# Four Strassen units moved ahead of the third block's up products, and second products of five groups by seven Strassen products

## The chip, the cores and the metric

The program runs on one core of a Trainium2 chip. The metric is the device time of one execution in microseconds (us), as a median of several runs. Inside the core, TensorE (PE) multiplies matrices into eight PSUM banks, VectorE (DVE) and ScalarE (ACT) read the banks and prepare operands, GpSimd (POOL) issues the accumulating transfers, and SyncE (SP) issues the other ones.

## The reference

The kernel computes one transformer block on x of 2048 tokens by 512 features in float32: layer norm with a modulation, an FNet mixing step, a gated residual, a second modulated layer norm (LN2), a SwiGLU with a hidden width of 1792, and a second gated residual. Cut to what matters here:

```python
h = layernorm(x) * (1 + scale1) + shift1
a, b = h @ dft_hid_re.T, h @ dft_hid_im.T
x = x + gate1 * (dft_seq_re @ a - dft_seq_im @ b)
h = layernorm(x) * (1 + scale2) + shift2
out = x + gate2 * ((silu(h @ w1) * (h @ w3)) @ w2)
```

The change touches only the last line and the order of the work around it.

## The kernel before, in words

Every float32 product is made of three matmuls on halves: each operand is split into a high half (a rounded copy, made on ACT by `copy`, line 87) and a low half (what the rounding left, made on DVE by `minus`, line 90), and `product` (line 98) issues high by high, high by low and low by high into one PSUM bank; all matmuls of the SwiGLU stand at line 100.

The tokens are cut into four blocks t of 512, which go in two pairs, (0, 2) and (1, 3). The hidden width is cut into seven groups of 256, each with its parts of w1, w3 and w2. So there are fourteen pieces of work, a group for a pair of blocks.

- Groups 0 and 1 of the first pair are done plainly. `up_block` (line 1076) issues 12 matmuls for one half of a group's columns and one block. It takes the banks 0 to 3 in turn. Block 0 comes first, then its second products, and then block 2, whose LN2 (`ln2`, line 817) has to be done by then.
- The other twelve pieces are `items` (line 1160): i = 0 to 4 are groups 2 to 6 of the first pair, i = 5 to 11 are groups 0 to 6 of the second pair. Their products with w1 and w3 are made by seven Strassen products each, called a1 to a7 (w1) and b1 to b7 (w3). `factor` (line 1239) issues one of them, six matmuls that may accumulate on in a bank that was already copied out; ACT (line 87) and DVE (line 93) take the partial results out. `weight_jobs` makes the sums of weight parts that the products need, and splits the weights and the sums into halves.
- `result` (line 1219) makes silu(a) times b and splits it into the tiles hf, of which there are four for a piece (two blocks by two halves of the columns).
- The second products (hf by w2) are made by `down_unit` (line 1115): for one block t and one of four output chunks d, six matmuls into a bank. ACT scales the bank by the gate into half of a tile y (line 335), and for every second chunk POOL issues a DMA that adds y, 512 KB, to the tile `sums[t, d // 2]` in the chip's memory (line 1146). The slot of y is given back four units later. That makes four such DMAs for a piece.
- For groups 5 and 6 of the second pair no y is made: `load_sums` (line 1103) has read the sums back into the tiles xr through SP, DVE adds the bank into xr (line 1137), and after group 6 SP stores xr as the output (line 1141). `load_sums` stands at the end of the second products of group 4 of the second pair, for one block after the other.

The order of the units is written out as strings in the loop over `items` (lines 1656 to 1670): "a6" is a unit of this item, "-b7" one of the item before, and "y" takes the next second product from the queue `seconds`. For most items it is

```python
body = "a6 a5 y a7 y y a4 y a3 y b1 y b2 y b6 b5 y"
head = "-b7 a1 -b4 -b3 a2 " if i == turning else "-b7 a1 a2 -b4 -b3 " if i else "a1 a2 "
```

`unit` (line 1621) and `down` (line 1579) issue one unit each, and with some of them loads of the next weights (`load_w`, line 1032, on SP). After each unit, `beside` (line 1566) takes steps from the queue `jobs` (weight splits and sums), and from `background` (LN2, the sums of LN2's parts) when `jobs` is empty, as far as DVE and ACT are thought to have time. `drain` (line 132) takes steps until a named one is done; `behind` (line 1063) puts something off by so many units. Each engine works through its instructions in the order in which they were issued. Tiles come from 50 slots of 512 KB that are taken first in, first out. `judge` (line 1003) is a short test on DVE of the inputs, 12 small instructions.

Of the kernel before, what the change touches and what calls it, by code (L numbers as in the profile page):

```python
# [42 lines left out]
def folded(nc, pools, c, cp, wmr, wmc, x, xt, ctr, cti, wdr, wdi, w1, w3, w2, out):  # L43
# [1032 lines left out]
    def up_block(g, t, q, w):  # L1076
        if q == 0 and w == "w1":
            drain(lambda: ("h2", t, 1) in done)
        to = bank(turn[0] % 4)
# [33 lines left out]
    down_banks = [4, 4]  # L1113

# [49 lines left out]
    def weight_jobs(i, w):  # L1164
# [30 lines left out]

        step(jobs, 1, highs, 0.0, 1.0)
        step(jobs, 1, totals, 1.4)
        step(jobs, 1, lows, 1.2)
        step(jobs, 1, sum_highs, 0.0, 1.0)
# [9 lines left out]
    state, vs = {}, {}  # L1209

# [8 lines left out]
    def result(i, w, q, k, src):  # L1219
# [6 lines left out]
        times(v, v, src)  # L1226

# [9 lines left out]
        behind(2, lows)  # L1237

    def factor(i, w, n):
# [37 lines left out]
        if n == 3:  # L1277
            for x in wuse.pop(key).values():
                give(x)
            behind(1, lambda: give(st["x"]))  # L1280
            if w == "w3":
                for x in vs.pop(i):
                    behind(3, lambda x=x: give(x))
# [295 lines left out]
    def down(g, pair, t, d, key):  # L1579
        drain(lambda: (key, "l") in done, jobs)  # L1580
        delayed()
        down_unit(g, pair, t, d, key)
        beside(1.36, USED["own" if pair == 1 and g >= NG - 2 else "y"])

    for w in ("w1", "w3"):
        load_w((w, 1))
        plain_jobs((w, 1))
    up(0, 0)
    for g in range(2):
        load_w(("w2", g))  # L1590
        plain_jobs(("w2", g))
    up(1, 0)
    load_w(("w1", *items[0]))
    for g in range(2):
        for d in range(ND):
            down(g, 0, 0, d, ("w2", g))
    judge()
    up(0, 2)
    load_w(("w3", *items[0]))
    weight_jobs(0, "w1")  # L1600
    up(1, 2)
    for h in (h2h, h2l):
        give(h.pop((2, 0)))


    down_banks[:] = [6, 2]
# [13 lines left out]

    def unit(kind, i, n):
        g, pair = items[i]
        more = i + 1 < len(items)
        if n == 1:
            drain(lambda: ("ready", i, "w1" if kind == "a" else "w3") in done, jobs)
# [8 lines left out]
        if (kind, n) == ("a", 1) and more:  # L1634
            load_w(("w1", *items[i + 1]))
        if (kind, n) == ("a", 6):
            load_w(("w2", g, pair))
        if (kind, n) == ("a", 3) and more:
            load_w(("w3", *items[i + 1]))
            weight_jobs(i + 1, "w1")  # L1640
        if (kind, n) == ("b", 2):
            plain_jobs(("w2", g, pair))
        if (kind, n) == ("b", 3):
# [7 lines left out]
            if more:  # L1651
                weight_jobs(i + 1, "w3")
            for t in PAIRS[pair]:
                seconds.extend((g, pair, t, d, ("w2", g, pair)) for d in range(ND))
        beside(1.36, FACTOR[kind][n])

    weight_jobs(0, "w3")
    ln2(1)
    ln2(3)
    for i in range(len(items)):  # L1660
        body = "a6 a5 y a7 y y a4 y a3 y b1 y b2 y b6 b5 y"
        if i == turning:
# [3 lines left out]
        head = "-b7 a1 -b4 -b3 a2 " if i == turning else "-b7 a1 a2 -b4 -b3 " if i else "a1 a2 "  # L1666
# [813 lines left out]
```

## Time and profile before

| | us |
|---|---|
| median of 3 runs | 711.03 |
| lowest and highest run | 710.54, 712.84 |
| the profiled execution's own time | 708.46 |
| its span, first to last instruction | 706.7 |
| PE busy | 686.3 (97% of the span) |
| DVE busy | 548.3 (78%) |
| ACT busy | 430.8 (61%) |
| POOL busy | 119.4 (17%) |

The page's time is that of one profiled execution; it lies 2.57 us under the median of the runs. PE's busy time includes matmuls at a lower clock; the mean granted clock over the span is 0.991. The duration of one matmul in the rows includes its filling and draining, and matmuls overlap: the pitch from one start to the next is what counts for a sum. The SwiGLU's Strassen part begins near 320 us and lasts to the end.

### The profile page before, as it was taken

The page shows a single profiled execution, that of the slowest core. Times are in us where ns is not written, and L with a number is a line of the kernel's source. Part 1 is how long each engine was busy: PE and PEld are TensorE (multiplying, and loading weights), DVE is VectorE, ACT ScalarE, POOL GpSimd, SP SyncE. Part 2 cuts the span into 40 slices and gives each one's busy share as a digit, 9 for nine tenths or more (in the row PEclk, how much of TensorE's full clock was granted, in tenths as well). Part 3 has the DMA queues.
Part 4 walks back from the last instruction along what each step waited for, and adds up shares of the span by engine and source line. Part 5 has one row for each costly group of instructions (what it writes and reads, how often), then busy time and mean ns, then how long its engine had stood idle before and what let it go on. Part 6 is the DMA issues. An engine that isn't in the chain of part 4 may idle for free.

```text
span 706.7 us, 8912 instructions
## 1 busy us (share of the span) xinstructions
PE 686.3 (97%) x3152; PEld 564.7 (80%) x3152; DVE 548.3 (78%) x877; ACT 430.8 (61%) x709; POOL 119.4 (17%) x141
## 2 busy tenths in 40 slices
PE   7999999999999999899999999999999999999995
PEld 4898888888888888687888788787788888888784
DVE  5999679997999978579987886896865556664763
ACT  4998865545454655745677676867665565656420
POOL 1320253542524000200100101011010100101000
PEclk9999999999999999999999999999999999999998
DMA  8730299796678521522868558376763847537403
GB/s 266 211 120 1 77 373 328 251 307 229 207 283 287 168 86 41 92 58 64 209 114 199 89 130 153 61 156 137 239 136 73 180 62 175 111 69 162 137 0 124
DMA packets 38100, 108.93 MB, mean 154 GB/s; under 512 B 4896, under 2 KB 5152, under 8 KB 38048
## 3 DMA queue, kind: packets, MB, share of 16 engines
q0 software_dynamic: 12352, 43.00, 29.3%
q1 hardware_dynamic: 25264, 63.98, 27.5%
q10 hardware_dynamic: 432, 1.31, 0.5%
q8 instruction: 26, 0.43, 0.3%
q14 instruction: 26, 0.21, 0.1%
HBM read 76.81 MB, written 33.55 MB: 156 GB/s over the span
## 4 chain that ended last, share of the span: by engine, by line
PE 81%; DVE 7%; ACT 6%; issue 2%; DMA 2%; SPq 1%; ACTq 0%; DVEq 0%
PE bank L100 52%; PE bank L750 25%; PE bank L559 2%; PE bank L598 1%; DMA wmr<-in_wmr 1%; ACT xc L894 1%; PE bank L576 1%; DVE xc L96 1%; SPq L231 1%; ACT hf L87 1%; ACT y L335 1%; DVE v L96 0%; DVE hl L90 0%; ACT hm L501 0%; DMA w<-in_wdi 0%
## 5 line engine op out<-in xcount | busy, mean ns | idle before, releaser
L100 PE MATMUL bank<-hf,w2h 128*128 128x512 f32 (+1 forms) x452 | 140.9, 391 | 0.3
L1146 POOL DMA_DIRECT2D sum<-y x48 | 41.0, 855 | 390.1 <-ACT y L335 373.0
L100 PEld LDWEIGHTS bank<-hf,w2h 128*128 128x128 f32 x452 | 84.3, 188 | 22.1 <-DVE hf L90 3.4
L100 PE MATMUL bank<-hf,w2l 128*128 128x512 f32 (+1 forms) x226 | 87.6, 388 | 0.0
L87 ACT ACTIVATE hf<-v 128x512 fp32r<-128x512 f32 x56 | 35.3, 630 | 67.3 <-DVE v L96 62.7
L335 ACT ACTIVATE y<-bank,gb 128x512 f32<-128x512 f32 x96 | 64.9, 682 | 18.6 <-PE bank L100 18.3
L93 DVE TENSOR_TENSOR v<-bank,x 128x512 f32<-128x512 f32 x36 | 24.7, 685 | 34.9 <-PE bank L100 34.8
L750 PE MATMUL bank<-bh,us 128*128 128x512 f32 x128 | 49.9, 390 | 0.0
L93 DVE TENSOR_TENSOR x<-bank,x 128x512 f32<-128x512 f32 x36 | 24.7, 687 | 32.4 <-PE bank L100 28.7
L750 PE MATMUL bank<-bh,ul 128*128 128x512 f32 x128 | 49.8, 389 | 0.0
L750 PE MATMUL bank<-d,us 128*128 128x512 f32 x128 | 49.8, 389 | 0.0
L750 PE MATMUL bank<-d,uh 128*128 128x512 f32 x128 | 49.8, 389 | 0.0
L750 PE MATMUL bank<-l,us 128*128 128x512 f32 x128 | 49.8, 389 | 0.0
L750 PE MATMUL bank<-l,uh 128*128 128x512 f32 x128 | 49.8, 389 | 0.0
L100 PEld LDWEIGHTS bank<-hf,w2l 128*128 128x128 f32 x226 | 42.4, 188 | 8.4
L90 DVE TENSOR_TENSOR hf<-v,hf 128x512 fp32r<-128x512 f32 x56 | 38.5, 687 | 12.2 <-ACT hf L87 12.1
L170 POOL DMA_INDIRECT re<-in_ctr,mirror x32 | 35.8, 1117 | 66.2 <-DVE ul L90 39.5
L1224 ACT ACTIVATE v<-v 128x512 f32<-128x512 f32 x36 | 22.8, 632 | 38.8 <-DVE v L93 38.8
L87 ACT ACTIVATE x<-bank 128x512 f32<-128x512 f32 x72 | 41.4, 586 | 7.2 <-PE bank L100 6.5
L170 POOL DMA_INDIRECT im<-in_cti,mirror x32 | 32.7, 1023 | 35.3 <-PE bank L750 10.0
L100 PE MATMUL bank<-h2h,w1h 128*128 128x512 f32 x80 | 31.8, 397 | 1.5 <-ACT h2h L87 1.5
L100 PE MATMUL bank<-h2l,w1h 128*128 128x512 f32 x80 | 31.9, 399 | 0.8 <-DVE h2l L90 0.8
(246 smaller groups left out, 1775.2 us busy)
## 6 DMA issues: line engine op xcount, KB each, us to landing
sum<-y POOLq DMA_DIRECT2D x48, 512.0 KB, 5.6
w<-in_w SPq DMA_DIRECT2D x42, 512.0 KB, 4.5
re<-in_ctr SPq DMA_DIRECT2D x32, 256.0 KB, 5.0
im<-in_cti SPq DMA_DIRECT2D x32, 256.0 KB, 5.0
wmc<-in_wmc SPq DMA_DIRECT2D x8, 512.0 KB, 6.3
xr<-in_xt SPq DMA_DIRECT2D x8, 512.0 KB, 7.6
sum<-xr SPq DMA_DIRECT2D x8, 512.0 KB, 6.2
x<-in_x SPq DMA_DIRECT2D x11, 256.0 KB, 4.8
```

What stands on the lines that cost most here:

```text
L87: nc.scalar.activation(dst, src, AF.Copy, scale=scale)
L90: nc.vector.tensor_tensor(out=dst, in0=a, in1=b, op=OP.subtract)
L93: nc.vector.tensor_tensor(out=dst, in0=a, in1=b, op=OP.add)
L96: nc.vector.tensor_tensor(out=dst, in0=a, in1=b, op=OP.mult)
L100: nc.tensor.matmul(acc, lhs[a], rhs[b], start=first and n == 0, stop=last and n == len(PASSES) - 1, skip_group_check=more,)
L170: nc.gpsimd.indirect_dma_start(dst, None, rows, bass.IndirectOffsetOnAxis(ap=at, axis=0))
L231: queue.dma_start(raw_w[dt][q * 64 : (q + 1) * 64, m, :], w[i][par::2, q])
L335: nc.scalar.activation(dst, src, AF.Identity, scale=by)
L559: nc.tensor.matmul(halves(hb[k])[:, m, :], sides((hh, hl)[a][k])[:, dt, m, :], wu[dt][:, b, m, :], start=False, stop=dt % 2 == 1 and n == ...
L750: nc.tensor.matmul(acc[what, e], lhs, rhs, start=begin and i == 0, stop=(end or (turn and what == "x")) and i == len(terms) - 1, skip_grou ...
L1146: nc.gpsimd.dma_start(sums[t, d // 2], y, accum_op=OP.add)
L1224: behind(k != 0 or q == 0, lambda: nc.scalar.activation(v, src, AF.Silu))
```

## The change

It has two parts. First, the units a1, a2, b1 and b2 of the first Strassen item are issued ahead of the up products of block 2, with w1's and w3's raw halves made early and the sums of weight parts later; `judge` comes after them, and the up products of block 2 take the banks 1, 2, 4 and 5. Second, for groups 0 to 4 of the second pair (`SEVEN`, i = 5 to 9) the second products of both blocks are made by seven Strassen products of six matmuls (`seven_unit`) instead of eight units of six. Each of the seven writes two banks, 6 and 7 (three matmuls each); four of them (3, 6, 7 and 4) accumulate on in the same two banks after ACT copied them out. Each of the seven gives one y and one accumulating DMA. The operands need four more subtractions on DVE and seven split tiles instead of four (`seven_parts`), and sums of parts of w2 (`seven_jobs`).

The order strings change with it: the seven products of an item stand two units apart. The w3 jobs of the items ahead of a `SEVEN` item follow b6 instead of b3. `load_sums` for both blocks now stands after the last of the seven products of group 4, which is in the head of the last item. The core of the diff:

```diff
+    def seven_parts(i, q, k):
...
+        t1, t2, t3, t4 = v[0, 0], v[1, 1], v[0, 1], v[1, 0]
+        behind(1, lambda: minus(t1, v[0, 1], v[0, 0]))
+        behind(2, lambda: high(5, t1))
+        behind(2, lambda: minus(t3, v[1, 1], v[0, 1]))
+        behind(3, lambda: low(5, t1))
+        behind(3, lambda: minus(t2, v[1, 1], t1))
+        behind(4, lambda: high(7, t3))
+        behind(4, lambda: minus(t4, v[1, 0], t2))
...
+    def seven_unit(g, pair, n, key):
+        new = n in (1, 2, 5)
+        if new:
+            banks7[:] = [bank(6), bank(7)]
+        y = take(F32, "y")
...
+        for e, to in enumerate(banks7):
+            at = int(LEFT7[n][1]) * HALF + e * P
+            product(
+                to,
+                [flat(wuse[key][x])[:, at : at + P] for x in names],
+                [u[:, b, :] for b in range(2)],
+                new,
+                True,
+                not new,
+            )
+            d = 2 * which + e
+            copy_by(y[:, e, :], to, gb[:, d : d + 1])
+        give(u)
+        nc.gpsimd.dma_start(sums[t, which], y, accum_op=OP.add)
+        behind(4, lambda: give(y))
...
+            if g == NG - 3:
+                for t in PAIRS[pair]:
+                    load_sums(t)
...
+    for at in ("a1", "a2", "b1", "b2"):
+        unit(at[0], 0, int(at[1]))
     judge()
+    up_banks[:] = 1, 2, 4, 5
+    down_banks[:] = [6, 2]
     up(0, 2)
...
         body = "a6 a5 y a7 y y a4 y a3 y b1 y b2 y b6 b5 y"
+        if i and items[i - 1] in SEVEN:
+            body = "a6 a5 a7 y a4 a3 y b1 b2 y b6 b5 y"
+        spread = i > 1 and items[i - 2] in SEVEN
+        if spread and i < len(items) - 1:
+            body = body.replace("a6", "a6 y", 1)
...
-            body = "a6 a5 y a7 y y a4 y a3 b1 y b2 b6 b5 y b7 y b4 y b3 y y y y y y y y"
...
+            body = "a6 a5 a7 a4 a3 b1 b2 y b6 y b5 y b7 y b4 y y b3 y y y y y y y y y y"
...
+        if spread and i < len(items) - 1:
+            head = "-b7 a1 y a2 -b4 y -b3 "
+        if i == len(items) - 1:
+            head = "-b7 y a1 a2 y -b4 -b3 y "
```

How the order of instructions moves at three places follows. In these rows a name's first number counts tiles, and the x at the end says how many instructions one row stands for.

First DVE, at LN2 of block 2, before:

```order
L90 TENSOR_TENSOR hf_379_2737<-v_377_2714,hf_379_2737 128x512
L883 RECIPROCAL s_2_377_2721<-s_2_377_2721 32x16
L847 COPY w_2_382_2753<-s_2_377_2721 32x16 x4
L848 STREAM_TRANSPOSE stat_347_2556<-w_2_382_2753 128x512
L96 TENSOR_TENSOR xc_348_2564<-xc_348_2564,stat_347_2556 128x1024
L96 TENSOR_TENSOR xc_360_2611<-xc_360_2611,stat_347_2556 128x1024
L90 TENSOR_TENSOR h2l_393_2821<-xc_348_2564,h2h_392_2819 128x1024
```

and now (w1l and w3l are the low halves of the first Strassen item's weights):

```order
L90 TENSOR_TENSOR hf_379_2737<-v_377_2714,hf_379_2737 128x512
L90 TENSOR_TENSOR w1l_388_2774<-w1_380_2740,w1h_387_2772 128x1024
L90 TENSOR_TENSOR w3l_391_2787<-w3_381_2742,w3h_390_2785 128x1024
L883 RECIPROCAL s_2_377_2721<-s_2_377_2721 32x16
L847 COPY w_2_391_2790<-s_2_377_2721 32x16 x4
L848 STREAM_TRANSPOSE stat_347_2556<-w_2_391_2790 128x512
L96 TENSOR_TENSOR xc_348_2564<-xc_348_2564,stat_347_2556 128x1024
L96 TENSOR_TENSOR xc_360_2611<-xc_360_2611,stat_347_2556 128x1024
L93 TENSOR_TENSOR v_400_2846<-bank1_402_2849,x_399_2845 128x512
L90 TENSOR_TENSOR h2l_404_2859<-xc_348_2564,h2h_403_2857 128x1024
L90 TENSOR_TENSOR h2l_408_2873<-xc_360_2611,h2h_407_2871 128x1024
```

The two weight splits now stand ahead of the reciprocal, and one addition of a Strassen unit stands ahead of the first low half of block 2.

Then ACT at the same place, now, from the last scaled copies of block 0 on (h2h are the high halves of block 2; line 1252 is the silu of a Strassen item):

```order
L335 ACTIVATE y_395_2815<-bank7_397_2827,gb_152 128x512
L894 ACTIVATE xc_360_2611<-xc_360_2611,sb_150,cb1_151 128x512 x2
L87 ACTIVATE x_399_2845<-bank0_398_2838 128x512
L87 ACTIVATE h2h_403_2857<-xc_348_2564 128x1024
L1252 ACT_TABLE_LOAD
L1252 ACTIVATE v_400_2846<-v_400_2846 128x512
L87 ACTIVATE x_406_2869<-bank3_405_2862 128x512
L87 ACTIVATE h2h_407_2871<-xc_360_2611 128x1024
```

Before, nothing but one scaled copy stood between the two h2h; now a table load, a silu and a copy of a Strassen unit do.

Last, the queue of SP near the end, before:

```order
L1106 DMA xr_903_5645<-sum_1_0_3300 128x1024
L1106 DMA xr_904_5646<-sum_1_1_3302 128x1024
L1035 DMA w3_905_5656<-in_w3 128x1024
L1106 DMA xr_925_5749<-sum_3_0_3799 128x1024
L1106 DMA xr_926_5750<-sum_3_1_3801 128x1024
L1035 DMA w2_937_5818<-in_w2 128x1024
```

and now:

```order
L1035 DMA w3_934_5753<-in_w3 128x1024
L1106 DMA xr_968_5933<-sum_1_0_3380 128x1024
L1106 DMA xr_969_5934<-sum_1_1_3382 128x1024
L1106 DMA xr_970_5937<-sum_3_0_3831 128x1024
L1106 DMA xr_971_5938<-sum_3_1_3833 128x1024
L1035 DMA w2_974_5953<-in_w2 128x1024
```

All four reads of the sums now stand together, after the last w3 and directly ahead of the last w2, the one of group 6. On DVE the low half of that w2 stands ahead of the first addition into xr:

```order
L90 TENSOR_TENSOR w2l_982_6009<-w2_974_5953,w2h_981_6007 128x1024
L1138 SCALAR_TENSOR_TENSOR xr_968_5933<-bank6_984_6013,gb_152,xr_968_5933 128x512
L90 TENSOR_TENSOR hf_983_6011<-v_959_5874,hf_983_6011 128x512
L1138 SCALAR_TENSOR_TENSOR xr_968_5933<-bank7_985_6029,gb_152,xr_968_5933 128x512
L1138 SCALAR_TENSOR_TENSOR xr_969_5934<-bank6_988_6046,gb_152,xr_969_5934 128x512
```

Here bank6 is used again by the third of the units whose results are added into xr.

## Rows read from the trace of the kernel before

**Rows 1.** The page, busy time of each engine over the span.
```profile
PE 686.3 (97%) x3152; PEld 564.7 (80%) x3152; DVE 548.3 (78%) x877; ACT 430.8 (61%) x709; POOL 119.4 (17%) x141
```

**Rows 2.** The critical chain, 225 to 320 us: start, duration, what.
```profile
262.54 21.77 PE bank L100 x96
...
297.97 22.07 PE bank L100 x90
```

**Rows 3.** PE's timeline, 294 to 325 us: start, duration, what, count [idle before].
```profile
294.80 0.39 PE L100 MATMUL bank<-hf,w2l 128*128 128x512 f32 x1
296.71 0.51 PE L100 MATMUL bank<-h2h,w1h 128*128 128x512 f32 x1 [1.53 <-ACT h2h L87]
297.97 0.79 PE L100 MATMUL bank<-h2l,w1h 128*128 128x512 f32 x1 [0.76 <-DVE h2l L90]
...
301.96 0.40 PE L100 MATMUL bank<-h2h,w3h 128*128 128x512 f32 x1
...
324.11 0.50 PE L100 MATMUL bank<-th,w1sh 128*128 128x512 f32 x1 [0.23 <-ACT x L87]
```

**Rows 4.** Windows: stretch, us, busy PE, PEld, DVE, ACT, POOL, clock, DMA.
```profile
28.00:29.00 1.00, 0.30 (x3) 0.10 (x1) 0.94 (x5) 1.00 (x3) 0.84 (x2) 1.00 0.61 201
298.00:299.00 1.00, 1.00 (x3) 0.81 (x4) 0.79 (x1) 0.98 (x2) 0.37 (x1) 0.50 0.97 193
547.46:577.63 30.17, 30.17 (x134) 24.70 (x133) 17.85 (x27) 18.25 (x28) 3.40 (x5) 1.00 0.60 122
```

**Rows 5.** ACT's timeline around LN2 of block 2.
```profile
287.29 1.82 ACT L335 ACTIVATE y<-bank,gb 128x512 f32<-128x512 f32 x3
290.49 1.53 ACT L894 ACTIVATE xc<-xc,sb,cb 128x512 f32<-128x512 f32 x2 [1.37 <-issue]
295.61 1.05 ACT L87 ACTIVATE h2h<-xc 128x1024 fp32r<-128x1024 f32 x1
298.20 1.28 ACT L1094 ACT_TABLE_LOAD   x1
```

**Rows 6.** DVE's timeline: around LN2 of block 2, and from 660 to 666 us.
```profile
287.42 0.24 DVE L883 RECIPROCAL s<-s 32x16 f32<-32x16 f32 x1 [0.93 <-ACT s L880]
289.18 2.36 DVE L96 TENSOR_TENSOR xc<-xc,stat 128x1024 f32<-128x1024 f32 x2
296.69 1.23 DVE L90 TENSOR_TENSOR h2l<-xc,h2h 128x1024 fp32r<-128x1024 f32 x1 [5.15 <-ACT h2h L87]
...
660.97 0.42 DVE L93 TENSOR_TENSOR w3s<-w 128x256 f32<-128x256 f32 x1
...
665.91 0.74 DVE L1137 SCALAR_TENSOR_TENSOR xr<-bank,gb,xr 128x512 f32<-128x512 f32 x1
```

**Rows 7.** Groups by shape, 547.46 to 577.63 us: count, busy, mean ns, idle before.
```profile
L335 ACT ACTIVATE y<-bank,gb 128x512 f32<-128x512 f32 x9 | 6.2, 685 | 2.3 <-PE bank L100 2.3
L90 DVE TENSOR_TENSOR hf<-v,hf 128x512 fp32r<-128x512 f32 x4 | 2.7, 686 | 0.7 <-ACT hf L87 0.7
L87 ACT ACTIVATE hf<-v 128x512 fp32r<-128x512 f32 x4 | 2.5, 634 | 4.6 <-DVE v L96 3.4 <-issue 1.3
```

**Rows 8.** Accumulating transfers, 288 to 345 us, from issue to landing.
```profile
DMA to landing us min/median/max: 5.3/5.6/8.6
```

**Rows 9.** POOL's timeline near the end.
```profile
653.82 0.85 POOL L1146 DMA_DIRECT2D sum<-y  x1 [5.95 <-ACT y L335]
```

**Rows 10.** SP's DMA queue, 659 to 661 us.
```profile
659.62 0.32 SPq L1106 DMA_DIRECT2D xr<-sum  x1
660.04 0.38 SPq L1035 DMA_DIRECT2D w<-in_w  x1
```

**Rows 11.** DMA issues, 659 to 661 us: count, KB each, us to landing.
```profile
xr<-sum SPq DMA_DIRECT2D x1, 512.0 KB, 3.6
w<-in_w SPq DMA_DIRECT2D x1, 512.0 KB, 4.4
```

**Rows 12.** ACT's timeline at the last w2.
```profile
674.33 1.05 ACT L87 ACTIVATE w2h<-w 128x1024 fp32r<-128x1024 f32 x1
```

More of the change, by code (lines that the diff above doesn't have):

```diff
@@ new lines, in seven_jobs, with highs, totals, lows @@
+    def seven_jobs(key):
+        use = wuse[key] = {}
+        def highs():
+            use["h"] = take(F32R, "w2h")
+            copy(flat(use["h"]), flat(wraw[key]))
+        def totals():
+            use["s"] = take(F32, "w2s")
+            s, r = four(use["s"]), four(wraw[key])
+            plus(s[:, 0, :], r[:, 1, :], r[:, 3, :])
+            minus(s[:, 1, :], s[:, 0, :], r[:, 0, :])
+            minus(s[:, 2, :], r[:, 0, :], r[:, 1, :])
+            minus(s[:, 3, :], r[:, 2, :], s[:, 1, :])
+        def lows():
+            use["l"] = take(F32R, "w2l")
+            r = wraw.pop(key)
+            minus(flat(use["l"]), flat(r), flat(use["h"]).bitcast(F32))
+            give(r)
+        def sum_highs():
+            use["sh"] = take(F32R, "w2sh")
+            copy(flat(use["sh"]), flat(use["s"]))
+        def sum_lows():
+            use["sl"] = take(F32R, "w2sl")
+            minus(flat(use["sl"]), flat(use["s"]), flat(use["sh"]).bitcast(F32))
+            give(use.pop("s"))
+            done.add((key, "l"))
+        step(jobs, 1, highs, 0.0, 1.0)
+        step(jobs, 1, totals, 1.4)
+        step(jobs, 1, lows, 1.2)
+        step(jobs, 1, sum_highs, 0.0, 1.0)
+        step(jobs, 1, sum_lows, 1.2)
@@ L1577, in up, with down @@
                 beside(2.72, USED[w])
-    def down(g, pair, t, d, key):
+    def down(g, pair, *which):
+        key = which[-1]
         drain(lambda: (key, "l") in done, jobs)
         delayed()
-        down_unit(g, pair, t, d, key)
+        if (g, pair) in SEVEN:
+            seven_unit(g, pair, *which)
+        else:
+            down_unit(g, pair, *which)
         beside(1.36, USED["own" if pair == 1 and g >= NG - 2 else "y"])
[L1585 to L1606, printed above, removed]
     seconds = deque((g, 0, 2, d, ("w2", g)) for g in range(2) for d in range(ND))
@@ L1623, in unit @@
         more = i + 1 < len(items)
-        if n == 1:
-            drain(lambda: ("ready", i, "w1" if kind == "a" else "w3") in done, jobs)
+        w = "w1" if kind == "a" else "w3"
+        if n == 1 or (i, n) == (0, 6):
+            need = ("raw", w) if (i, n) == (0, 1) else ("ready", i, w)
+            drain(lambda: need in done, jobs)
         if (kind, i, n) == ("a", 0, 6):
@@ L1633, in unit @@
         factor(i, "w1" if kind == "a" else "w3", n)
-        if (kind, n) == ("a", 1) and more:
+        if (kind, n) == ("a", 1 if i else 6) and more:
             load_w(("w1", *items[i + 1]))
@@ L1637, in unit @@
             load_w(("w2", g, pair))
[L1638 removed]
+        if (kind, n) == ("a", 7 if i == turning else 3) and more:
             load_w(("w3", *items[i + 1]))
             weight_jobs(i + 1, "w1")
[L1641 to L1642 removed]
+        if (kind, n) == ("b", 2 if i else 6):
+            (seven_jobs if (g, pair) in SEVEN else plain_jobs)(("w2", g, pair))
         if (kind, n) == ("b", 3):
@@ L1650, in unit @@
                 other_operands()
-            if more:
+            if more and not early_w3(i):
                 weight_jobs(i + 1, "w3")
-            for t in PAIRS[pair]:
-                seconds.extend((g, pair, t, d, ("w2", g, pair)) for d in range(ND))
-        beside(1.36, FACTOR[kind][n])
-    weight_jobs(0, "w3")
+            if (g, pair) in SEVEN:
+                seconds.extend((g, pair, n, ("w2", g, pair)) for n in ORDER7)
+            else:
+                for t in PAIRS[pair]:
+                    seconds.extend((g, pair, t, d, ("w2", g, pair)) for d in range(ND))
+        if (kind, n) == ("b", 6) and more and early_w3(i):
+            weight_jobs(i + 1, "w3")
+        beside(1.36, FACTOR[kind][n])
+    for w in ("w1", "w3"):
+        load_w((w, 1))
+        plain_jobs((w, 1))
+    up(0, 0)
+    for g in range(2):
+        load_w(("w2", g))
+        plain_jobs(("w2", g))
+    up(1, 0)
+    for w in ("w1", "w3"):
+        load_w((w, *items[0]))
+        weight_jobs(0, w)
+    for g in range(2):
+        for d in range(ND):
+            down(g, 0, 0, d, ("w2", g))
+    for at in ("a1", "a2", "b1", "b2"):
+        unit(at[0], 0, int(at[1]))
+    judge()
+    up_banks[:] = 1, 2, 4, 5
+    down_banks[:] = [6, 2]
+    up(0, 2)
+    sum_jobs("w1")
+    up(1, 2)
+    for h in (h2h, h2l):
+        give(h.pop((2, 0)))
+    sum_jobs("w3")
     ln2(1)
```

61 lines of the change are left out of this document (58 added, 3 removed).

## The prediction, made before the changed kernel was run

> **What bounds the kernel now.** I read the busy time of the engines first: PE works for 97% of the span [rows 1], so the time is nearly the number of matmuls by their pitch, plus the places where PE waits. The chain of waits confirms this: both long pieces of it around LN2 of block 2 are matmuls at line 100 [rows 2]. The first of them gives the pitch, 21.77 / 96 = 0.2268 us for a matmul, 1.36 us for a unit of six. PE's timeline then shows where PE waits in the SwiGLU: at one place for long, between the second products of block 0 and the up products of block 2, and later only for small pieces such as the 0.23 us at 324.11 [rows 3]. The windows by stage show one group of the second pair, 30.17 us in which PE never rests while DVE works for 17.85 us and ACT for 18.25 [rows 4]. So in that stage a matmul less is time won, as long as DVE and ACT keep up.
>
> **Base.** The sum is made against the profiled execution (708.46 us, span 706.7). It lies 2.57 us under the median of the runs, 711.03. I carry the difference over to the median. A measurement of this kernel can tell about 0.3% from no change, which is 2.1 us here: below 708.9 is faster, above 713.2 slower.
>
> **Term 1, matmuls.** Eight units of six become seven in five groups: 5 x 6 = 30 matmuls fewer. At 0.2268 us [rows 2] that is **-6.8 us**. PE has no idle time in a group of the second pair [rows 4], so all of it counts if nothing new makes PE wait.
>
> **Term 2, LN2 of block 2.** Before, the last matmul of the second products starts at 294.80, and the 13th of the up products, the first with w3h, at 301.96 [rows 3]. Without any wait that one would start at 294.80 + 13 x 0.2268 = 297.75. So 4.2 us are lost there. Some 2.7 of them are idle (1.68 ahead of the first matmul, 1.03 ahead of the second), and 1.5 the clock: the 11 matmuls from 297.97 took 3.99 us instead of 2.49 [rows 3], under a granted clock of 0.50, which is the lower of its two levels, 1.2 GHz; it fell after the first wait [rows 4].
>
> The change gives PE 24 matmuls more ahead of that wait, 5.4 us, to 300.5. But the LN2 is late too. The two splits w1l and w3l now stand ahead of the reciprocal on DVE, and each waits for its high half on ACT. ACT's three scaled copies end at 289.1 [rows 5]. Then come w1h (1.05, as for the equally large h2h [rows 5]), a scaled copy of 0.6, and w3h until 291.6; DVE's w3l (1.23, as for the equally large h2l) ends at 292.9, and the reciprocal follows at 292.9 instead of 287.42 [rows 6]. From there the two products with the statistics begin 1.7 us later and last 2.36 [rows 6]; ACT's scalings (0.76 each), with one copy of y and one of x between, end at 299.9, and the first h2h at 300.9, its low half at 302.2. On ACT the table load (1.28 [rows 5]), a silu and a copy of x now stand ahead of the second h2h, which ends at 304.3, and its low half at 305.6. The up products need these at their 1st, 2nd, 7th and 8th matmul. So the 8th starts at 305.6, where it could have been at 302.05: 3.55 us are lost, in pieces of 0.5 to 1.0. Whether the clock falls for such pieces, no row shows exactly: it did after 1.68 us, at a cost of 1.5, and did not after 0.70 us in one us [rows 4]. I take 0.5, because the pieces are nearest to the second row, with 0 and 1.5 as ends. With the 0.23 at 324.11, which goes since a1 is done early, the term is 3.55 + 0.5 - 4.2 - 0.2 = **-0.4 us**, between -0.9 and +0.8. The first part of the change moves the gap rather than closing it. The splits cost nothing by themselves; they are work that stood later.
>
> **Term 3, the groups with seven products.** PE needs 30.17 x 126/132 = 28.8 us for such a group. DVE gets three more low halves and four subtractions (0.686 each, [rows 7]), four sums of w2's parts (0.42 each, as for w3s [rows 6]) and a split of 1.23: 17.85 + 7.7 = 25.5 us, 89%. ACT gets six scaled copies (0.685), three high halves (0.634) [rows 7] and one of 1.05: 18.25 + 7.1 = 25.3 us, 88%. Neither becomes the bound, but the slack shrinks from 12 us to 3.5. The products stand two units apart, so both banks have 2.72 us to be copied out, in which ACT needs 1.37 and what stands ahead. I followed the order of ACT and DVE against PE's through one group at these durations: the tightest place, bank 6 between products 6 and 7, has some 0.4 us to spare, and at the first such item DVE is some 0.8 us late with the sum after a7, for which a4 waits. I take 0.8 + 4 x 0.1 = **+1.2 us**, with ends 0 (all hidden) and +3. The three accumulating transfers more for a group are behind nothing that PE waits for, unless a y's slot is missing: it is given back four units after the issue, 5.4 us, taken again later, and transfers landed after 5.6, at worst 8.6 us [rows 8].
>
> **Term 4, the last item.** Here the change adds a wait. The four reads of the sums now follow the last seven product of group 4, and the load of the last w2 is queued behind them on SP. Let z be the end of that product on PE. ACT has a high half ahead, then copies both banks until z + 2.1; POOL issues y. The second read, of `sum_1_1`, needs it landed: before, a y issued at 653.82 released such a read at 659.62 [rows 9, 10], 5.8 us later, so z + 7.9 here. Behind it stand two more reads and w2, issued 0.42 apart [rows 10]. A read lands after 3.6 us and a w2 issued 0.42 behind it after 4.4, so they land 1.22 us apart [rows 10, 11]: w2 lands at z + 7.9 + 3.6 + 3 x 1.22 = z + 15.2. Then w2h on ACT, 1.05 [rows 12], its low half on DVE, 1.23, and only then, in DVE's order, the first addition into xr, 0.74 [rows 6], which frees bank 6: z + 18.2. PE wants that bank for the third unit of its kind, whose place is eleven units after z, 15.0 us. So PE waits 3.2 us, and the clock falls as it did after 1.68 us, 1.5 more: **+4.8 us** (ends 1.5, if the reads run side by side and the clock holds, and 6). Before, the same w2 landed at 660.04 + 4.4 = 664.4 and was first used at 674.33 [rows 10 to 12]: 10 us to spare, all of which go.
>
> The Trainium skill, DMA: Bandwidth & Descriptors, section Anatomy of one DMA, gives for a transfer issued by the other path about 2.0 us plus bytes by 436 KB per us. By it, as an estimate, four of 512 KB in a row would take 6.8 us instead of 7.3, PE would wait 0.5 less, and the sum be 0.5 lower. The rows are of the queue in question and decide.
>
> **Sum.** -6.8 - 0.4 + 1.2 + 4.8 = -1.2 us, which gives 709.8. With all ends low it is -6.8 - 0.9 + 0 + 1.5 = -6.2 (704.8), all high +3.0 (714.0). The forecast's own range is 707.4 to 712.2.
>
> **Rivals.**
> - The tail hides its wait: the reads of the sums don't hold w2 up that long, or DVE's order leaves the addition in front. Terms 1 to 3 remain, -6.0: **705.0**. For it: the 5.8 us between issue and read may hold a wait of SP for something else. Against: SP's queue in the order of the change has w2 last. Chance 0.22.
> - The gap at LN2 closes altogether, for instance if DVE's splits run before the reciprocal's wait is over: 3.9 us better than term 2 at most, the rest as forecast: **705.7**. Against: w3h stands behind four scaled copies on ACT. Chance 0.06.
> - Slower: the two banks of the seven products are not emptied in time. All seven use banks 6 and 7, and four go on in the very bank that ACT has just read. If one weight split of 1.05 us more than I foresee stands ahead of the copies at two products of a group, PE waits 2 x (1.05 - 0.4) = 1.3 us in each of the four steady groups: 5.2, so +4.0 and **715.0**. It decides from about 0.9 us a group on. For it: ACT and DVE at 88 to 89%. Against: the spacing of two units. Chance 0.14. The Trainium skill, Perfetto Trace Analysis, section Matmuls, speaks for this rival: independent groups of matmuls should rotate through banks so that one's evacuation lies beside the next one's matmuls. By it every group would pay some such wait; no row of before shows a second product going on in a bank just copied.
> - The forecast: 0.58, of which faster 0.20, same 0.34, slower 0.04.
>
> **Numbers.** Faster 0.20 + 0.22 + 0.06 = 0.48; same 0.34 + 0.02 of the slower rival = 0.36; slower 0.04 + 0.12 = 0.16. The range is 704.8 to 714.0: it takes in both faster rivals and the high end, and leaves out most of the slower one.
>
> **What would show it.** In the profile after: 1848 matmuls at line 100 instead of 1878; the reciprocal near 292.9 and matmuls of the first up unit in pieces until 306; a group of 28.8 to 29.2 us with PE full; a wait of about 3 us on DVE at line 1138 with w2l before it, in the last 35 us, and a clock below 1.00 there. I am wrong if PE runs through the last item, if the group is over 29.7 us, or if the up products start without a wait.

## The result, and the profile after

The changed kernel takes 712.99 us (median of 22 runs, 708.80 to 715.38), the kernel before 710.20 us (22 runs beside them, 708.27 to 712.84). The ratio is 1.0032, with a 95% interval from 1.0022 to 1.0043: slower, by some 2.3 us (the two medians lie 2.8 apart; the changed kernel's runs spread more widely). The forecast was 1.2 us faster.

Three rows of the page of the changed kernel answer to [rows 1]: the number of matmuls fell by 30, and PE's share of the span fell with it, so PE waits more.

```profile
span 711.1 us, 9006 instructions
...
PE 681.3 (96%) x3122; PEld 558.9 (79%) x3122; DVE 582.8 (82%) x937; ACT 454.9 (64%) x759; POOL 132.3 (19%) x156
...
PEclk9999999999999999999999999999999999999998
```

To see where the time went, one can follow the matmuls of the SwiGLU one by one. The first up product and the last second product are these, in PE's timeline of the kernel before (start, duration, what):

```profile
262.38 0.39 PE L100 MATMUL bank<-h2h,w1h 128*128 128x512 f32 x1
...
698.47 0.28 PE L100 MATMUL bank<-hf,w2l 128*128 128x256 f32 x1
```

and in that of the changed kernel, with those of the waits between them on which the readings below rest (the idle time ahead of a matmul and what ended it stand in brackets):

```profile
263.99 0.39 PE L100 MATMUL bank<-h2h,w1h 128*128 128x512 f32 x1
...
303.63 0.50 PE L100 MATMUL bank<-h2l,w1h 128*128 128x512 f32 x1 [0.76 <-DVE h2l L90]
305.74 0.50 PE L100 MATMUL bank<-h2h,w1h 128*128 128x512 f32 x1 [0.69 <-ACT h2h L87]
307.00 0.50 PE L100 MATMUL bank<-h2l,w1h 128*128 128x512 f32 x1 [0.76 <-DVE h2l L90]
...
334.81 0.73 PE L100 MATMUL bank<-hf,w2h 128*128 128x512 f32 x2 [0.54 <-ACT y L335]
336.94 0.50 PE L100 MATMUL bank<-th,w1h 128*128 128x512 f32 x1 [0.47 <-DVE v L93]
...
344.62 0.74 PE L100 MATMUL bank<-hf,w2h 128*128 128x512 f32 x2 [0.58 <-ACT y L335]
...
515.65 0.50 PE L100 MATMUL bank<-th,w1h 128*128 128x512 f32 x1 [1.04 <-DVE v L93]
...
564.95 0.73 PE L100 MATMUL bank<-hf,w2sh 128*128 128x512 f32 x2 [0.16 <-ACT y L335]
...
659.77 0.50 PE L100 MATMUL bank<-th,w1sh 128*128 128x512 f32 x1 [0.68 <-ACT x L87]
662.28 0.50 PE L100 MATMUL bank<-th,w1h 128*128 128x512 f32 x1 [0.85 <-DVE v L93]
677.78 1.22 PE L100 MATMUL bank<-hf,w2h 128*128 128x512 f32 x2 [4.33 <-DVE xr L1138]
...
702.76 0.28 PE L100 MATMUL bank<-hf,w2l 128*128 128x256 f32 x1
```

So the SwiGLU takes 436.09 us before and 438.77 after, 2.68 more. (The 1.61 us by which it starts later belong to a part of the program that the change doesn't touch; the last section returns to them.) Thirty matmuls at 0.2267 us are 6.80 us less, so 9.48 us more are lost. For each stretch, the lost time is the time between the starts of its first matmul and of the next stretch's, less the number of its matmuls times 0.2267 us:

| stretch | lost before, us | lost after, us | difference |
|---|---|---|---|
| LN2 of block 2, to the ninth up product | 4.19 | 3.44 | -0.75 |
| the rest up to the end of the first Strassen item | 0.73 | 2.50 | +1.77 |
| the other items of the first pair, up to the first units of the second | 4.06 | 2.38 | -1.68 |
| up to the second of the seven products (the wait at 515.65 is in it) | 0.77 | 1.32 | +0.55 |
| from there on, the groups with seven products | 0.96 | 3.01 | +2.05 |
| the last item | -0.17 | 7.37 | +7.54 |

The loss includes idle time, the slower start of a matmul after it and the lower clock; in the last item, matmuls of half the width make it a little less. The rows above show the places. The long wait of [rows 3] became three short ones at the 2nd, 7th and 8th up product, as forecast, and three waits in the first Strassen item (334.81 to 344.62) are new. A group with seven products costs little (0.16 to 0.25 us of wait at bank 6 in each). The row at 677.78 is the one that decides: PE waits 4.33 us for the first addition into xr, 4.5 with the slower start of its first matmul. The chain behind it, backwards, is in four views. DVE's timeline (the first two rows are from LN2 of block 2, for a later section):

```profile
291.70 1.23 DVE L90 TENSOR_TENSOR w1l<-w,w1h 128x1024 fp32r<-128x1024 f32 x1 [3.60 <-ACT w1h L87]
...
294.37 0.23 DVE L883 RECIPROCAL s<-s 32x16 f32<-32x16 f32 x1
...
675.83 1.23 DVE L90 TENSOR_TENSOR w2l<-w,w2h 128x1024 fp32r<-128x1024 f32 x1 [5.94 <-ACT w2h L87]
676.98 0.75 DVE L1138 SCALAR_TENSOR_TENSOR xr<-bank,gb,xr 128x512 f32<-128x512 f32 x1
```

ACT's timeline:

```profile
674.75 1.06 ACT L87 ACTIVATE w2h<-w 128x1024 fp32r<-128x1024 f32 x1 [7.46 <-DMA w<-in_w]
```

SP's queue, with the three later reads in one row, and POOL's, with the last accumulating transfer:

```profile
653.84 0.33 SPq L1106 DMA_DIRECT2D xr<-sum  x1
...
665.86 1.27 SPq L1106 DMA_DIRECT2D xr<-sum  x3
...
667.23 0.38 SPq L1035 DMA_DIRECT2D w<-in_w  x1
```

```profile
658.58 0.85 POOL L1360 DMA_DIRECT2D sum<-y  x1 [3.89 <-DVE hf L90]
```

The transfer issued at 658.58 holds the second read until 665.86: SP's queue does nothing between the two rows, and its wait there was ended by that transfer. The w2 behind it is issued at 667.23, is there at 674.75, is split by 677.0, and the addition that frees bank 6 comes last. Then the clock: windows, with PE's busy time after the length of the stretch and the granted clock in the third column from the end; the first two are groups with seven products.

```profile
535.70:564.95 29.25, 29.09 (x126) 23.49 (x126) 24.81 (x40) 23.16 (x38) 5.97 (x7) 1.00 0.91 180
564.95:594.04 29.09, 28.93 (x126) 23.50 (x127) 24.82 (x40) 23.17 (x38) 5.96 (x7) 1.00 0.88 175
676.00:677.00 1.00, 0.00 (x0) 0.00 (x0) 1.00 (x2) 1.00 (x3) 0.00 (x0) 1.00 0.00 0
677.00:678.00 1.00, 0.22 (x1) 0.22 (x2) 1.00 (x3) 0.29 (x1) 0.00 (x0) 0.66 0.00 0
678.00:679.00 1.00, 1.00 (x3) 0.81 (x4) 0.98 (x2) 0.00 (x0) 0.00 (x0) 0.50 0.08 16
681.00:682.00 1.00, 1.00 (x6) 0.79 (x5) 0.50 (x1) 0.00 (x0) 0.00 (x0) 1.00 0.00 0
```

After the wait PE works at 1.2 GHz (0.50) for three more us, at which some 1.5 us are lost.

### The profile page after: what moved, and what is told of

Read it like the earlier page. It is cut to its first block, busy times and chain, and to the rows that moved or that the text cites. A ratio compares the mean times of both kernels' runs of the same rounds, so it can differ in the third digit from the quotient of the medians.

```text
span 711.1 us, 9006 instructions
## 1 busy us (share of the span) xinstructions
PE 681.3 (96%) x3122; PEld 558.9 (79%) x3122; DVE 582.8 (82%) x937; ACT 454.9 (64%) x759; POOL 132.3 (19%) x156
## 4 chain that ended last, share of the span: by engine, by line
PE 69%; DVE 12%; ACT 10%; issue 4%; DMA 3%; another core or an unknown queue 1%; POOL 0%; SPq 0%; ACTq 0%; DVEq 0%; POOLq 0%
PE bank L100 40%; PE bank L750 24%; PE bank L559 2%; ACT y L335 2%; DVE v L96 1%; DMA w<-in_w 1%; PE bank L598 1%; ACT x L87 1%; ACT hf L87 1%; ACT w3sh L87 1%; DVE x L93 1%; DVE xr L805 1%; DMA sum<-y 1%; DVE v L93 1%; DMA x<-in_x 1%
## 5 line engine op out<-in xcount | busy, mean ns | idle before, releaser
L100 PE MATMUL bank<-hf,w2h 128*128 128x512 f32 (+1 forms) x352 | 109.7, 393 | 5.7 <-DVE xr L1138 4.3
L87 ACT ACTIVATE hf<-v 128x512 fp32r<-128x512 f32 x71 | 44.3, 630 | 71.8 <-DVE v L96 59.6
L335 ACT ACTIVATE y<-bank,gb 128x512 f32<-128x512 f32 x126 | 81.5, 681 | 8.1 <-PE bank L100 8.1
L100 PEld LDWEIGHTS bank<-hf,w2h 128*128 128x128 f32 x352 | 65.8, 189 | 22.4 <-DVE xr L1138 5.1
L1147 POOL DMA_DIRECT2D sum<-y x28 | 24.0, 857 | 246.9 <-ACT y L335 233.6
L100 PE MATMUL bank<-hf,w2l 128*128 128x512 f32 (+1 forms) x176 | 68.6, 390 | 0.0
L90 DVE TENSOR_TENSOR hf<-v,hf 128x512 fp32r<-128x512 f32 x71 | 48.4, 687 | 11.2 <-ACT hf L87 11.0
L1360 POOL DMA_DIRECT2D sum<-y x35 | 29.8, 852 | 133.6 <-ACT y L335 115.1
L93 DVE TENSOR_TENSOR v<-bank,x 128x512 f32<-128x512 f32 x36 | 24.7, 687 | 24.8 <-PE bank L100 18.6
L100 PEld LDWEIGHTS bank<-hf,w2l 128*128 128x128 f32 x176 | 33.3, 189 | 6.8
```

What stands on the lines that cost most here:

```text
L87: nc.scalar.activation(dst, src, AF.Copy, scale=scale)
L90: nc.vector.tensor_tensor(out=dst, in0=a, in1=b, op=OP.subtract)
L93: nc.vector.tensor_tensor(out=dst, in0=a, in1=b, op=OP.add)
L100: nc.tensor.matmul(acc, lhs[a], rhs[b], start=first and n == 0, stop=last and n == len(PASSES) - 1, skip_group_check=more,)
L335: nc.scalar.activation(dst, src, AF.Identity, scale=by)
L1147: nc.gpsimd.dma_start(sums[t, d // 2], y, accum_op=OP.add)
```

## The experiments

Each run is compared with runs of the kernel before on the same chip. Since the start of the program varies, the length of the SwiGLU (first up product to start of the last matmul, as above; 436.09 before, 438.77 after) is given beside the ratio.

### The last w2 ahead of the reads

```diff
             if g == NG - 3:
+                load_w(("w2", NG - 1, pair))
                 for t in PAIRS[pair]:
                     load_sums(t)
```

> The changed kernel, with the load of the last group's w2 issued on SP's queue directly ahead of the four reads of the sums instead of behind them. Theory (that load, held back behind the reads that wait for the last accumulating transfer, makes PE wait 4.3 us at the first addition into xr, and the lower clock after it costs some 1.5 us more): both go, w2 is there before it is wanted; about 6 us less than the changed kernel, ratio to the kernel before about 0.995 (0.993 to 0.997), no wait of PE over 1 us after 665 us into the program. Rival (the wait moves on to the reads themselves, since the additions need xr, or DVE's order holds bank 6 in any case): ratio 1.000 or more, and a wait of 2 us or more at the same unit.

Measured: ratio 0.9970 (0.9958 to 0.9983), SwiGLU 433.83 us, 4.94 less than the changed kernel. In PE's timeline after 655 us these two waits are all that is left:

```profile
660.96 0.50 PE L100 MATMUL bank<-th,w1sh 128*128 128x512 f32 x1 [0.68 <-ACT x L87]
663.60 0.50 PE L100 MATMUL bank<-th,w1h 128*128 128x512 f32 x1 [0.98 <-DVE v L93]
```

The wait at the addition is gone, and so is the lower clock. The ratio came out 0.2% above what was expected: the wait (4.5 us with its first matmul) and the clock (1.5) went as said, but in this run the groups with seven products lost 0.9 us more and the a4 of the last item 0.1 more. The program is the same in those groups, so single traces of these kernels differ by about as much. This edit alone turns the change from slower into faster. So w2's place behind the reads is what cost the change its gain.

### The first part alone

```diff
-    SEVEN = [(g, 1) for g in range(NG - 2)]
+    SEVEN = []
...
-        if (kind, n) == ("a", 7 if i == turning else 3) and more:
+        if (kind, n) == ("a", 3) and more:
...
-            body = "a6 a5 a7 a4 a3 b1 b2 y b6 y b5 y b7 y b4 y y b3 y y y y y y y y y y"
+            body = "a6 a5 y a7 y y a4 y a3 b1 y b2 b6 b5 y b7 y b4 y b3 y y y y y y y y"
...
-        if i == len(items) - 1:
-            head = "-b7 y a1 a2 y -b4 -b3 y "
```

> The first part alone: a1, a2, b1 and b2 of the first Strassen item ahead of the up products of block 2, everything from the second pair on as in the kernel before. Theory (LN2 of block 2 becomes late with the splits ahead of the reciprocal, so the gap there shrinks by only 0.8 us, and the first item pays 1.8 us in new waits, while the two items after it win back some 1 us): ratio 1.000, between 0.998 and 1.002. Rival (the moved units close the gap at LN2 for good): a ratio of 0.995.

Measured: ratio 0.9986 (0.9975 to 0.9997), SwiGLU 435.42 us, 0.67 less than before. It has the waits of the changed kernel to a hundredth at LN2 and in the first item, and that of the kernel before from the second pair on. The first part gains almost nothing, as expected: what LN2 gives, the first item takes back, and the items after it lose less (-1.68 in the table), for a reason that these runs don't show.

### The second part alone

```diff
-    for at in ("a1", "a2", "b1", "b2"):
-        unit(at[0], 0, int(at[1]))
     judge()
-    up_banks[:] = 1, 2, 4, 5
+    up(0, 2)
+    load_w(("w3", *items[0]))
+    weight_jobs(0, "w1")
+    up(1, 2)
     down_banks[:] = [6, 2]
-    up(0, 2)
-    sum_jobs("w1")
-    up(1, 2)
```

The jobs of the first item and its order string are those of the kernel before as well.

> The second part alone: seven second products in five groups of the second pair, with the order of the kernel before up to the end of the first pair. Theory (30 matmuls fewer, -6.8 us; new waits in the five groups +2.7; the last item +7.6 us, since the last w2 comes late): +3 us, ratio 1.004, between 1.002 and 1.006. Rival (the first part is what makes the changed kernel slower): a ratio below 1.000.

Measured: ratio 1.0034 (1.0010 to 1.0059). The profiled execution was the longest of its runs (716.16; their median is 714.13), with a SwiGLU of 442.10 us, in the main since the lower clock lasted longer after the wait of the last item, to 685 us, at which 3.0 us were lost in place of 1.5; the wait is again 4.48 us with its first matmul. The slowdown belongs to the second part.

### The first item's splits behind LN2's chain

```diff
     up(1, 0)
     for w in ("w1", "w3"):
         load_w((w, *items[0]))
-        weight_jobs(0, w)
     for g in range(2):
         for d in range(ND):
             down(g, 0, 0, d, ("w2", g))
+            if (g, d) == (0, 3):
+                weight_jobs(0, "w1")
+                weight_jobs(0, "w3")
```

> The changed kernel, with the high halves and splits of the first Strassen item's w1 and w3 queued after the fourth second product of block 0 instead of ahead of all eight, so that on DVE the reciprocal and the products with the statistics stand ahead of w1l and w3l again, and on ACT both h2h stand ahead of the table load. Theory (the splits ahead of the reciprocal are what keeps the gap at LN2 open): the waits of 0.76, 0.69 and 0.76 us at the up products of block 2 go but for some 0.3 us, 2 to 3 us less than the changed kernel, ratio about 0.9995 (0.998 to 1.001). Rival (LN2's chain is late by itself, through ACT, which has the same two high halves in the way): waits of 2 us or more there, ratio 1.003.

Measured: ratio 1.0004 (0.9988 to 1.0020), SwiGLU 434.27 us, 4.50 less than the changed kernel. Of the three waits at LN2 one of 0.94 us is left, and of the three in the first item two of 0.24 and 0.54; up to the groups with seven products 3.3 us are won, most of the rest lies in the last item, where PE waited 3.3 instead of 4.5 us. The 0.94 us have another cause than the waits that went: the up products take bank 1, which DVE reads for the sum of a2 only after the first low half of block 2. DVE's timeline shows the reciprocal ahead of the splits again:

```profile
288.43 0.24 DVE L883 RECIPROCAL s<-s 32x16 f32<-32x16 f32 x1 [0.93 <-ACT s L880]
...
295.15 1.23 DVE L90 TENSOR_TENSOR w1l<-w,w1h 128x1024 fp32r<-128x1024 f32 x1 [2.60 <-ACT w1h L87]
```

In the changed kernel, by the rows of its DVE timeline above, w1l runs at 291.70 and the reciprocal only at 294.37. So the splits' place is what kept the gap at LN2 open. The edit moves their halves on ACT and on DVE together, so it doesn't show how much each of the two orders cost.

### Both edits, and two further ones

Both edits together, without any other:

> Both edits together: the last w2 loaded ahead of the reads of the sums, and the first item's splits queued after the fourth second product of block 0. Theory (the two waits are independent: 4.9 us were won at the last item by the one, 3.6 us up to there by the other in the traces): 8 us less than the changed kernel, ratio to the kernel before 0.992 (0.990 to 0.994). Rival (what is won at LN2 is lost again later, since DVE and ACT are the limit of the later stages): 0.995 or more.

Measured: ratio 0.9945 (0.9926 to 0.9963), SwiGLU 430.68 us, 8.1 less than the changed kernel. The ratio is 0.05% above the expected range, and its interval takes in the rival's 0.995, so the ratio alone doesn't decide. The trace does: 3.3 us are won up to the groups with seven products, as with the late splits, and 6.0 in the last item, where w2 first had won 5.9. So the two waits are independent. The groups, in which the program is the same, lost 1.3 us more in this trace.

```diff
     def early_w3(i):
-        return items[i] in SEVEN
+        return items[i] in SEVEN or i == len(items) - 2
```

> As the run with both edits, and the splits and sums of the last item's w3 are queued after b6 of the item before instead of after its b3, as the changed kernel does for the items with seven products. Theory (the waits of 0.84 and 1.0 us at a7 and a4 of the last item come from w3sh on ACT and w3l and w3sl on DVE, which stand ahead of the copy after a6 and of the sum after a7): both go, 1.9 us less, ratio 0.989. Rival (the 4.1 us of DVE work and 2.1 us of ACT work, now in a piece ahead of the sum after b7, make b4 or a second product wait as long there): ratio as with both edits, 0.992.

Measured: ratio 0.9925 (0.9908 to 0.9942), SwiGLU 430.52 us: 0.16 less than without the edit, so the rival; the difference of the two ratios is no larger than their intervals allow. The wait at a7 of the last item went, but a second product now waits, and the one at a4 stays:

```profile
645.59 0.73 PE L100 MATMUL bank<-hf,w2sh 128*128 128x512 f32 x2 [0.89 <-ACT y L335]
...
660.43 0.50 PE L100 MATMUL bank<-th,w1h 128*128 128x512 f32 x1 [0.84 <-DVE v L93]
```

DVE was idle ahead of that last sum and had nothing else to do. With a4 directly after a7, PE waits for the sum in any case; the w3 jobs are no part of it.

```diff
-            body = "a6 a5 y a7 y y a4 y a3 y y y b6 b5 y"
+            body = "a6 y a5 y a7 y a4 y a3 y y b6 y b5 y"
```

> As the run before, and in the first Strassen item the second products stand one for each other unit (a6 y a5 y a7 y a4 y a3 y y b6 y b5 y) instead of in pairs and a triple. Theory (the waits of 0.4 and 0.7 us at a4 and at the third second product in a row come from ACT's scaled copies of two banks standing behind each other): both go, some 1 us less, ratio 0.9875. Rival (they come from DVE's sums of w3 parts and the additions of LN2, which stay where they are): no change, ratio 0.989.

Measured: ratio 0.9938 (0.9921 to 0.9955), SwiGLU 431.27 us, 0.75 more than the run before. A miss: the wait for ACT's scaled copies went, but a4 waits 1.56 us, 0.24 in the run with the late splits, for the sum after a7, because one second product less lies between them, while DVE does four additions of the first gated residual (line 805) ahead of that sum.

### The seven products one unit apart

```diff
         if i and items[i - 1] in SEVEN:
-            body = "a6 a5 a7 y a4 a3 y b1 b2 y b6 b5 y"
-        spread = i > 1 and items[i - 2] in SEVEN
-        if spread and i < len(items) - 1:
-            body = body.replace("a6", "a6 y", 1)
+            body = "a6 a5 y a7 y a4 y a3 y b1 y b2 y b6 y b5"
...
-        if spread and i < len(items) - 1:
-            head = "-b7 a1 y a2 -b4 y -b3 "
-        if i == len(items) - 1:
-            head = "-b7 y a1 a2 y -b4 -b3 y "
```

> The changed kernel with the seven products one unit apart instead of two, all seven in the body of the item after. Theory (the spacing matters, since all seven use banks 6 and 7 and ACT needs 1.37 us for the two copies, plus what stands ahead, where only 1.36 us lie between): some 0.5 us of wait at most of the products, 2 to 4 us for a steady group against 0.8 in the changed kernel, 10 us over the stage; the last item's wait at the additions into xr shrinks by some 3 us since the reads come earlier; ratio 1.010 (1.005 to 1.015). Rival (ACT copies fast enough, the two banks are no limit): under 1.5 us a group, ratio 1.000 or less.

Measured: ratio 0.9985 (0.9973 to 0.9997), SwiGLU 432.36 us, 6.4 less than the changed kernel. The theory fell: the two banks are emptied in time with one unit between as well. From the first of the seven products to the last, 2.8 us are lost where the changed kernel loses 4.4, some 0.4 of them in each steady group; such a group takes as long as in the changed kernel (29.25 and 29.09 us in its windows above):

```profile
560.92:590.02 29.10, 29.00 (x127) 23.51 (x127) 24.75 (x40) 23.41 (x38) 5.97 (x7) 1.00 0.84 175
```

Since the last of the products now lies in the item before, SP's reads and w2 come earlier, and the wait at the additions is gone without any change of SP's queue. A wait of 2.74 us at a4 of the last item took its place, because that item has nothing for PE between a7 and a4, while DVE does the w3 jobs. The clock didn't fall after that wait, as the window behind it shows:

```profile
664.84 0.50 PE L100 MATMUL bank<-th,w1h 128*128 128x512 f32 x1 [2.74 <-DVE v L93]
...
664.00:668.00 4.00, 3.16 (x14) 2.63 (x15) 0.89 (x3) 1.23 (x2) 0.00 (x0) 1.00 0.48 188
```

### One unit apart, late splits, and the last item as before

```diff
-            body = "a6 a5 a7 a4 a3 b1 b2 y b6 y b5 y b7 y b4 y y b3 y y y y y y y y y y"
+            body = "a6 a5 y a7 y y a4 y a3 b1 y b2 b6 b5 y b7 y b4 y b3 y y y y y y y y"
```

on top of one unit apart and the late splits:

> The changed kernel with the seven products one unit apart, all seven in the body of the item after, the last item in the order of the kernel before (its own second products between the units), and the first item's splits queued after the fourth second product of block 0; the last w2 stays behind the reads of the sums. Theory (the product spacing of one is no limit; with the last seven product ahead of the last item, reads and w2 come early enough without a change of SP's queue; the wait of 2.7 us at a4 seen with one unit apart came from the w3 jobs on DVE, with nothing for PE to do between a7 and a4): no wait of PE over 1.3 us in the second pair or the last item, 2.7 us fewer lost than in the kernel before and 30 matmuls fewer, ratio 0.987 (0.984 to 0.990). Rival (waits of other kinds take their place in the last item): 0.992 or more.

Measured: **ratio 0.9855 (0.9839 to 0.9872)**, 699.85 us, SwiGLU 426.49 us, 9.6 less than before. It beats both kernels. 7.74 us are lost in all, 10.54 before, and no wait in the second pair or the last item is over 0.41 us. With w2 ahead of the reads as well:

> As the run before, with the last w2 loaded ahead of the reads of the sums as well. Theory (w2's place in the queue costs only where the reads are late; here w2 is wanted some 14 us after the last seven product or later anyway): no difference to the run before beyond 0.15%. Rival (the place of w2 costs by itself): 0.4% less or more.

Measured: ratio 0.9892 (0.9875 to 0.9908), neither the one nor the other: 0.37% more than the run before, where none or less was expected. But the SwiGLU takes 426.54 us, 0.05 from the run before; only the part ahead of it, in which the two programs don't differ, is longer, by 2.78 us. So both kernels once more, unedited:

> The kernel of the run with one unit apart and late splits, once more without any edit. In its trace the up products of the SwiGLU began at 263.3 us, in that of the run with w2 first as well at 266.1, though both programs are the same up to there, and the rest took 426.5 us in both. Theory (the first transfers of the program land up to 3 us later in some loadings of a program, drawn anew each time): this run may lie anywhere from 699 to 703 us, with the SwiGLU's 426.5 us unchanged. Rival (the build decides): 699.9 again, with a start of the SwiGLU at 263 to 264.

> The kernel of the run with one unit apart, late splits and w2 first, once more without any edit. Theory (the start is drawn anew with each loading): anywhere from 699 to 703 us, SwiGLU 426.5 us. Rival (the build decides): 702.5 again, with a start of the SwiGLU near 266.

Measured: 0.9859 (0.9842 to 0.9875), with the SwiGLU from 265.15 us on, 426.44 us long; and 0.9865 (0.9849 to 0.9882), from 263.39 on, 426.43 us long. The one start moved up by 1.85 us, the other down by 2.69. So the build doesn't set the start, and w2's place does not matter where the reads are early. Whether the start changes with the loading of a program or with each execution these runs don't separate: they were made on another chip than the two before them, and the profiled execution with the start at 265.15 took 701.60 us, the other three of that run 699.68 to 700.35.

## Why the prediction was wrong

The direction was wrong: 1.2 us faster was forecast, 2.3 slower measured, by a mechanism that the forecast had, at a price that was too small. In the SwiGLU, 2.7 us slower where 1.2 faster was forecast, term 4 makes 2.7 us of the miss and term 3 makes 1.4. By its terms:

- **Term 1** (-6.8) is right: 1848 matmuls, and a group of 29.1 to 29.25 us, as forecast (28.8 to 29.2).
- **Term 2** (-0.4) was nearly right: -0.75 at LN2, where the forecast, without the wait at 324.11, had -0.2. The reciprocal came 6.95 us later than in [rows 6], of which 1.61 are the later start; 5.5 had been forecast. The waits are the forecast's, at the forecast's matmuls but for the first; the clock stayed at 1.00 through them, where 0.5 us had been taken for it, and the first h2h came nearly in time. That the splits are the cause was shown by moving them. The rival in which this gap closes altogether (0.06) didn't come about.
- Not in the sum at all: three waits in the first Strassen item, +1.77, and the smaller loss in the items after it, -1.68. They cancel by chance, so they did no harm to the number.
- **Term 3** (+1.2, ends 0 and +3) was +2.6 (0.55 + 2.05), inside its ends. The first such item lost 1.04 us at a4, for 0.8 forecast; the rest are mostly waits of 0.16 to 0.25 at bank 6. DVE worked 24.8 us of 29.1 and ACT 23.2, for 25.5 and 25.3 forecast.
- **Term 4** (+4.8, ends 1.5 and 6) is the step that failed: it named the wait, its place and its chain, and measured +7.5, outside its ends. Three sizes in it were too small. The last accumulating transfer held the second read for 7.3 us (658.58 to 665.86), where the 5.8 of [rows 9, 10] had been taken: it was issued 4.7 us after the one before it, with the DMA engines busy (the share in the windows is 0.91 in a group, 0.60 in [rows 4]). Which of the two made it longer wasn't tried, and the kernel before had such a length as well: of its accumulating transfers from 640 us on the slowest landed after 7.1 us; the 5.8 belong to another one. The three reads and the w2 from there on took until 674.75, 8.9 us from the second read's issue, where 7.3 had been worked out from [rows 10, 11]. And the two waits at a7 and a4, 2.1 us with the slower starts that follow them, weren't seen: the last item had lost the second products that lay between these units. They put off the point where PE wants bank 6 as well, so the wait grew by 1.1 us, from 3.2 to 4.33, and not by 3.1. The clock's 1.5 us were as forecast.

Two small slips in the sums did no harm: term 2's high end is +0.65 by its own numbers and not +0.8, and the rival with the gap closed is 705.9 and not 705.7.

The Trainium skill, DMA: Bandwidth & Descriptors, section Anatomy of one DMA, has a fit for transfers that GpSimd issues; as an estimate, it would make the four transfers 6.8 us long. The trace's 8.9 lies further from it than from the rows' 7.3.

Of the rivals, that of the tail with no wait (0.22) is what one row of SP's queue makes of the kernel, at 0.9970. The slower rival, that the two banks aren't emptied in time (0.14), is excluded as a cause: it costs 0.16 to 0.25 us of wait in a group, 0.4 to 0.5 with the slower start behind it, and 0.4 with half the spacing. The Trainium skill, Perfetto Trace Analysis, section Matmuls, has independent matmuls rotate through banks so that one's evacuation lies beside the next one's matmuls; here one unit of 1.36 us in other banks was enough for that.

## What to carry to other kernels

A load that is queued behind reads which wait for late results is as late as they are, whatever it depends on itself (w2 was issued at 667.23 us behind the reads, at 650.69 ahead of them): look at every queue in which a step's reads move, and name what stands behind them. When work is taken out from between two dependent units (here the second products between a7 and a4), the wait that it covered appears; the cost of a moved unit is also what it used to hide. And a wait should be costed with the load on the queue at its new place, not with the duration it had where the queue was idle.

## What the runs showed of the hardware

The start of the program varies, by up to 4.6 us between the profiles here: the same instructions reached the SwiGLU at 262.38 us in the one of the kernel before and at 263.30 to 266.95 in those of the other kernels. Between the run with one unit apart and late splits and the one with w2 first, 2.25 of the 2.78 us are there at PE's first wait for hh, at 21.87 us in the one and 24.12 in the other. Some 1.0 us of that is there when PE begins on x (8.97 and 9.92 us), while the first loads land. The rest comes while the clock is lower; the stretch from 9 to 16 us, in the one and in the other:

```profile
9.00:16.00 7.00, 5.91 (x42) 5.04 (x43) 4.62 (x9) 3.40 (x7) 0.00 (x0) 1.00 1.05 293
...
9.00:16.00 7.00, 6.08 (x23) 4.93 (x24) 5.29 (x9) 3.95 (x7) 0.00 (x0) 0.51 1.05 304
```

The two profiles with the latest starts (266.08 and 266.95 us) are the two in which the granted clock was at the lower level for some 7 us within the first 20; in the others it was for 3.5 there or not at all. Two sets of runs of one kernel, on two chips, differed by 2.2 us in their medians (702.54 and 700.35), with each median's four runs within 1.7 us; the kernel before differed by 0.5 between these chips. So a ratio can be off by 0.3% though its runs agree, and the length of a stretch that both programs share is the better measure. What makes the first loads land later, and the clock fall in some executions only, wasn't tried.

The clock fell after 1.68 us of idle time ([rows 3, 4]) and after 4.33, and not in the stretch from 302 to 308 us of the changed kernel, in which PE waited three times for 0.69 to 0.76 us. Nor did it fall after the 2.74 us of the run with one unit apart (1.00 up to 668 us), or after the 1.56 us at a4 of the first item in the run with that item's order changed (1.00 from 333 to 339 us). So the length of one wait doesn't tell by itself whether the clock falls. After the wait of the last item it came back after 3 us in the changed kernel, but after some 6 in the run of the second part alone, which may be one reason why these two kernels' runs spread more (708.70 to 716.16 the latter) than those of the kernel before; no run shows it.
